# Splitting the gate and up signals of a fused attention and FFN kernel, with satisfied waits on two engines

## The chip, the cores and the metric

The kernel runs on one core of one Trainium2 chip. The metric is device time in microseconds of one execution; the *span* is the part from the first to the last instruction that the profile covers. I call reported time minus span the *surplus*. Spans are listed to 0.1 us for every run, so a surplus read from them is good to about 0.05 us.

## The reference, cut to what matters

```python
x = A_x                                              # [1, 2048, 640] bf16
g = sigmoid((x * gate_w).sum(-1, keepdims=True))
a = linear_attention(x, wqkv, w_phi, wo)             # 32 heads of 20, softmax features
b = (silu(x @ w_gate) * (x @ w_up)) @ w_down         # FFN width 1728
return g * a + (1 - g) * b
```

## The kernel before

The kernel is written by hand for five engines. A small tracker gives each engine one semaphore, lets every recorded operation raise it by one, and puts the waits that the data need ahead of an operation. A group of matmuls signals once, at its last one. A list of short codes fixes the order of all work.

The part that the change touches is one FFN item: the gate half and the up half of a 128-column block, each five matmuls of 512 columns into its own PSUM bank of a pair (PSUM: the `ps` tiles of the profile, into which the matmuls write). ScalarE takes the Tanh of the gate bank and copies the up bank, VectorE forms (tanh + 1) * gate, and POOL multiplies that with the copy.

```python
def fitem(bt, k):
    pr = next_pair()
    ...
    if k < 13:
        g, up = bank(2 * pr, 0, 512), bank(2 * pr + 1, 0, 512)
        mm(group(g, [(wg[:, c, P * k:P * k + P], xr[c]) for c in range(5)])
           + group(up, [(wu[:, c, P * k:P * k + P], xr[c]) for c in range(5)]))
        h = hT[:, buf, k, :]
    ...
    actop(h, g, ACTF.Tanh, 0.5)
    actop(u, up, ACTF.Copy)
    stt(h, h, 1.0, g, ALU.add, ALU.mult)
    tt("pool", h, h, u, ALU.mult)
```

`H` in the order is a pair of warm-up matmuls, `U` a part of a value tile, `M` premultiplies a block of the key weights (`wT`), `K` is a key projection, `N` ends the accumulation of keys times values, `Z` follows it.

The softmax here doesn't subtract the row's maximum and nothing guards it: scores larger than these inputs give would overflow.

## Time and profile before

| | before |
|---|---|
| time, median of 3 runs (range) | 289.55 us (289.07 to 290.51) |
| span of the profiled run | 288.40 us |
| TensorE busy | 285.0 us, 99% |
| last matmul starts | 286.30 us |
| first key projection to last matmul | 266.96 us |
| instructions of PE, of ScalarE | 4042, 300 |

The instruction counts take a matmul as two, weight load and multiply (1975 of each on the page). The stretch from the first key projection to the last matmul is the difference of two start times in the trace (19.34 and 286.30). The *tail* is the stretch from the start of the last matmul to the end of the span. The prediction shows the lines of this profile and how they are read.

### The profile page before, as it was taken

How to read it: one execution, taken by the hardware profiler on the slowest of the kernel's cores; microseconds unless marked ns; L12 is line 12 of the kernel's file. 1: busy time of each engine (PE TensorE's matmuls, PEld its weight loads, DVE VectorE, ACT ScalarE, POOL GpSimd, SP SyncE). 2: the span in 40 equal slices, each digit the busy share in tenths (PEclk: the TensorE clock that was granted, in tenths of full speed). 3: DMA queues.
4: the chain of work that ended last, by engine and by line, in shares of the span. 5: the costliest groups of instructions: out<-in, count | busy, mean ns of one | idle time of the engine just before them, and what ended most of it. 6: DMA issues, size and time to landing. Idle time of an engine off the chain costs nothing.

```text
span 288.4 us, 4897 instructions
## 1 busy us (share of the span) xinstructions
PE 285.0 (99%) x1975; PEld 174.6 (61%) x1975; DVE 162.6 (56%) x243; ACT 148.2 (51%) x252; POOL 160.4 (56%) x125
## 2 busy tenths in 40 slices
PE   8999999999999999999999999999999999999997
PEld 6667777575644445556775556675554446656776
DVE  2146748486468987669992385980317799200000
ACT  1468768676674556673355663225675452234112
POOL 8286899889545799835743348350653649601000
DMA  7975779000010497302383002061020004410101
GB/s 212 178 115 120 111 197 375 26 1 2 0 50 0 84 323 135 78 5 44 56 140 91 15 1 50 2 142 49 2 50 0 2 1 84 91 45 0 49 23 48
DMA packets 48943, 21.62 MB, mean 75 GB/s; under 512 B 39384, under 2 KB 48792, under 8 KB 48920
## 3 DMA queue, kind: packets, MB, share of 16 engines
q1 hardware_dynamic: 48190, 20.62, 31.4%
q10 hardware_dynamic: 730, 0.68, 0.7%
q8 instruction: 16, 0.26, 0.4%
q14 instruction: 7, 0.06, 0.1%
HBM read 9.29 MB, written 2.62 MB: 41 GB/s over the span
## 4 chain that ended last, share of the span: by engine, by line
PE 93%; SPq 4%; DMA 2%; issue 0%; DVE 0%
PE ps L294 93%; SPq L347 3%; DMA wT<-in_A_wqkv_dram 2%; SPq L348 1%; DVE osb L724 0%; PE ps L306 0%
## 5 line engine op out<-in xcount | busy, mean ns | idle before, releaser
L322 POOL TENSOR_TENSOR hT<-hT,us 128x512 bf16<-128x512 bf16 (+1 forms) x56 | 65.6, 1180 | 66.3 <-DVE hT L326 66.1
L326 DVE SCALAR_TENSOR_TENSOR hT<-hT,ps 128x512 bf16<-128x512 bf16 (+1 forms) x56 | 37.5, 683 | 73.0 <-ACT hT L312 60.7
L294 PE MATMUL ps<-xT,wg 128*128 128x512 bf16 x260 | 64.6, 379 | 0.0
L294 PE MATMUL ps<-xT,wu 128*128 128x512 bf16 x260 | 64.6, 379 | 0.0
L294 PE MATMUL ps<-wd,hT 128*128 128x320 bf16 (+2 forms) x462 | 63.9, 295 | 0.0
L312 ACT ACTIVATE hT<-ps 128x512 bf16<-128x512 f32 (+2 forms) x60 | 35.8, 596 | 46.6 <-PE ps L294 46.4
L322 POOL TENSOR_TENSOR ph<-eq,qc 128x1320 bf16<-128x1320 bf16 x16 | 42.3, 2646 | 26.1 <-DVE qc L632 24.0
L294 PEld LDWEIGHTS ps<-wd,hT 128*128 128x128 bf16 x462 | 44.5, 98 | 17.5 <-issue 0.2
L294 PE MATMUL ps<-wqk,xT 128*128 128x320 bf16 x320 | 47.7, 299 | 0.1
L294 PEld LDWEIGHTS ps<-xT,wu 128*128 128x128 bf16 x260 | 25.5, 98 | 30.7
L294 PEld LDWEIGHTS ps<-xT,wg 128*128 128x128 bf16 x260 | 25.1, 98 | 27.8 <-ACT oT L312 0.8
L312 ACT ACTIVATE osb<-ps,omg 128x640 bf16<-128x640 f32 (+2 forms) x17 | 12.9, 757 | 53.7 <-PE ps L294 53.7
L322 POOL TENSOR_TENSOR ekr<-ekr,krec 128x1280 bf16<-128x1280 bf16 x16 | 37.4, 2357 | 5.2 <-DVE krec L336 5.2
L294 PEld LDWEIGHTS ps<-wqk,xT 128*128 128x128 bf16 x320 | 30.6, 98 | 13.2 <-ACT us L312 0.5
L312 ACT ACTIVATE us<-ps 128x512 bf16<-128x512 f32 (+1 forms) x56 | 33.2, 594 | 0.3 <-POOL hT L322 0.2
L312 ACT ACTIVATE eq<-ps 128x640 bf16<-128x640 f32 x32 | 22.3, 703 | 17.3 <-POOL ph L322 10.4
L333 DVE TENSOR_REDUCE ksum<-ekr 128x64 f32<-128x1280 bf16 x16 | 23.5, 1470 | 11.2 <-ACT ekr L312 11.2
L312 ACT ACTIVATE ekr<-ps 128x640 bf16<-128x640 f32 x32 | 22.3, 703 | 8.2 <-PE ps L294 7.7
L333 DVE TENSOR_REDUCE qz<-eq 128x64 f32<-128x1280 bf16 x16 | 23.7, 1478 | 2.2 <-ACT eq L312 2.2
L294 PE MATMUL ps<-wvg,xT 128*128 128x320 bf16 (+1 forms) x160 | 24.4, 301 | 0.3 <-DVE xT L318 0.2
L294 PE MATMUL ps<-wog,oT 128*128 128x320 bf16 (+2 forms) x165 | 24.7, 295 | 0.0
L333 DVE TENSOR_REDUCE qw<-ez 128x64 f32<-128x1280 bf16 x16 | 23.6, 1476 | 0.0
(73 smaller groups left out, 188.4 us busy)
## 6 DMA issues: line engine op xcount, KB each, us to landing
out_dram<-osb SPq DMA_DIRECT2D x15, 160.0 KB, 1.9
wd<-in_B_w_down_dram SPq DMA_DIRECT2D x1, 2080.0 KB, 10.7
wg<-in_B_w_gate_dram SPq DMA_DIRECT2D x1, 1040.0 KB, 11.3
wu<-in_B_w_up_dram SPq DMA_DIRECT2D x1, 1040.0 KB, 11.5
wg<-in_B_w_gate_dram SPq DMA_DIRECT2D x1, 800.0 KB, 7.4
wu<-in_B_w_up_dram SPq DMA_DIRECT2D x1, 800.0 KB, 9.0
wog<-in_A_wo_dram SPq DMA_DIRECT2D x2, 375.0 KB, 7.3
wvg<-in_A_wqkv_dram SPq DMA_DIRECT2D x4, 160.0 KB, 4.1
```

What stands on the lines that cost most here:

```text
L294: last = pe.matmul(o, lhsT=l, rhs=r, start=st, stop=sp_, skip_group_check=sk)
L312: return run("act", lambda: act.activation(o, i, func, scale=scale), rd, [o])
L322: return run(e, lambda: eo.tensor_tensor(o, a, b, op), [a, b], [o])
L326: return run("dve", lambda: dve.scalar_tensor_tensor(out=o, in0=a, scalar=s, in1=b, op0=op0, op1=op1), rd, [o])
L333: return run("dve", lambda: dve.tensor_reduce(o, i, AX.X, ALU.add), [i], [o])
L347: return eo.dma_start_transpose(dst, src)
L348: return eo.dma_start(dst, src)
```

## The change

It does two things. The gate half of an FFN item now signals by itself, so that the Tanh need not wait for the up half. And waits that are already satisfied are put into the programs of ScalarE (88, code `a`) and PE (24, in `N`). They make the programs longer (on net, PE's from 4042 to 4046 instructions and ScalarE's from 300 to 360) and so shift the program fetches: the last packet of queue 8, which I take for PE's, began at 285.44 us before.

```diff
+NWAIT = 88
+NPEW = 24
-H0 H1 H2 H3 H4 H5 H6 H7 H8 H12 G ...
+H0 H1 a H2 H3 H4 H5 H6 H7 H8 H12 G ...
+    def act_waits():
+        for _ in range(NWAIT):
+            act.wait_ge(tr.sem["pe"], 1)
...
-            mm(group(g, [(wg[:, c, P * k:P * k + P], xr[c]) for c in range(5)])
-               + group(up, [(wu[:, c, P * k:P * k + P], xr[c]) for c in range(5)]))
             h = hT[:, buf, k, :]
+            mm(group(g, [(wg[:, c, P * k:P * k + P], xr[c]) for c in range(5)]))
+            mm(group(up, [(wu[:, c, P * k:P * k + P], xr[c]) for c in range(5)]))
...
     def kv_end():
+        for _ in range(NPEW):
+            pe.wait_ge(tr.sem["pe"], 1)
         kv_finish()
```

More of the change, by code (lines that the diff above doesn't have):

```diff
@@ L36 @@
 ORDER = """
-H0 H1 H2 H3 H4 H5 H6 H7 H8 H12 G X0 H9 H10 U0.0 X1 H11 U1.0 U0.1 U1.1 X2 U2.0 U0.2 U1.2 U2.1
+H0 H1 a H2 H3 H4 H5 H6 H7 H8 H12 G X0 H9 H10 U0.0 X1 H11 U1.0 U0.1 U1.1 X2 U2.0 U0.2 U1.2 U2.1
 X3 U2.2 U0.3 U1.3 U2.3 U0.4 U1.4 U2.4 V3 Y F0.1 M1 i3 M0 F0.0 M2 V4 M3 M4 K0 K1 I S0 V6 V5 S1 P0
@@ L744, in _build @@
         "f": lambda i: load_ffn(FCUT[i], FCUT[i + 1]), "L": load_late_weights, "T": tail_weights, "J": gates,
-        "Y": w_blocks, "I": kv_begin, "N": kv_end, "Z": z_row,
+        "Y": w_blocks, "a": lambda: act_waits(), "I": kv_begin, "N": kv_end, "Z": z_row,
         "Q": qtile, "A": qsum, "B": qden, "C": qscale, "c": qmul,
```

## The prediction

One paragraph is cut from the text where marked: statements about the hardware that go beyond what this case's runs show. The trace of before: 91 wait instructions on PE and 41 on ScalarE; sixteen packets of 16384 bytes on queue 8, which begin when 229 to 4005 of PE's instructions have started, 252 apart on average; packets of 8192 bytes on queue 14. The pace from which the text counts its 13 late steps, N/2.4 + 2.5 ns for N columns, is here a line through this trace's median steps: it is within 1 ns of them at 80, 96, 140, 224, 320 and 512 columns (35, 42.5, 61, 96, 136 and 216 ns) and 3 ns below them at 63 and 321. Of the three stretched issues named under (b), the one of 2.58 us is a plain load of gate weights and no transpose.

> **What bounds the kernel now.** I read the page from the top: busy shares, the slices, the queues, the chain that ended last.
>
> ```profile
> PE 285.0 (99%) x1975; PEld 174.6 (61%) x1975; DVE 162.6 (56%) x243; ACT 148.2 (51%) x252; POOL 160.4 (56%) x125
> ...
> PE   8999999999999999999999999999999999999997
> ...
> q8 instruction: 16, 0.26, 0.4%
> q14 instruction: 7, 0.06, 0.1%
> ...
> PE 93%; SPq 4%; DMA 2%; issue 0%; DVE 0%
> ```
>
> TensorE is busy 99% of the span, and no slice but the first and the last is below 9. The other engines are little more than half busy. The two instruction lines are the program fetches that the change wants to place. Busy TensorE can still be padded, so I cut the span at the two places where the chain changes hands and asked for busy time in each stretch:
>
> ```profile
> 0.00:19.00 19.00, 17.58 (x141) 12.05 (x141) 5.83 (x14) 8.00 (x17) 10.98 (x28) 1.00 0.82 175
> 19.00:286.50 267.50, 267.40 (x1834) 162.57 (x1834) 156.41 (x229) 140.17 (x237) 149.42 (x98) 1.00 0.29 68
> 286.50:288.40 1.90, 0.01 (x1) 0.00 (x0) 0.32 (x1) 0.00 (x0) 0.00 (x0) 1.00 0.19 45
> ```
>
> First number: length; second: TensorE busy. The middle 267.5 us are full. From the trace's start times, the median step from a 512-column matmul to the next is 216 ns and from a 320-column one 136 ns, and between 19 and 286.5 us only 13 steps are more than 15 ns over N/2.4 + 2.5 ns; their excess is 1.06 us in all. So this stretch has about 1 us to give. The chain in order of time shows what sets its two ends:
>
> ```profile
> 14.36 4.61 DMA wT<-in_A_wqkv_dram
> 18.97 0.05 issue
> 19.02 59.32 PE ps L294 x562
> ...
> 128.49 158.03 PE ps L294 x1020
> 286.52 0.02 issue
> 286.54 0.32 DVE osb L724
> ```
>
> The start is SyncE's row of transposing loads, whose last weight block lands at 18.97. The end is the eviction of the last 96 columns and their store: issued by ScalarE at 286.89, its semaphore complete at 288.35. The reported time is 289.64 for the profiled run against a span of 288.40; I carry that 1.24 us over unchanged.
>
> [...] the last fetch ran from 285.44 to 286.42, and of the store then under way (128x320) fifteen arrivals came by 286.11 and the sixteenth at 287.49.
>
> **The change part by part.**
>
> *Split signal.* No matmul is removed, added or moved; the order of matmuls, activations and vector operations is the same. The last gate matmul now signals too, so the Tanh of a gate bank may start 5 x 216 ns = 1.08 us earlier, while the up half runs. The first consumer of a pair frees its banks sooner. What is that worth? Only where TensorE waits for such a bank. Of the 13 steps, ten surround the attention output groups (about 95 ns before and after each, tied to waits for transposed phi and to switches of operand). One is 78 ns at 131.07, after a wait for oT. The largest, 239 ns, is an FFN bank:
>
> ```profile
> 127.03 0.60 ACT L312 ACTIVATE hT<-ps 128x512 bf16<-128x512 f32 x1 [0.72 <-PE ps L294]
> 127.52 0.59 ACT L312 ACTIVATE us<-ps 128x512 bf16<-128x512 f32 x1
> 127.66 0.69 DVE L326 SCALAR_TENSOR_TENSOR hT<-hT,ps 128x512 bf16<-128x512 bf16 x1 [0.70 <-ACT hT L312]
> ...
> 128.46 2.57 PEld L294 LDWEIGHTS ps<-wqk,xT 128*128 128x128 bf16 x20 [0.53 <-ACT us L312]
> ```
>
> The next projection wants the pair; VectorE's product with the gate bank ends at 127.66 + 0.69 = 128.35, and the weight load starts 0.11 us later. With the split, this Tanh starts after the two activations that end near 126.3, not at 127.03; the product is then done by about 127.6 and the 0.24 us go. TensorE has no slack behind it, so they reach the end: **-0.24 us**. The new waits are cheap: the us copies get their own wait for PE, 16 of them as extra instructions on ScalarE, executed while its Tanh of 596 ns runs: 0.
>
> *88 waits on ScalarE.* In the built program two waits share one instruction, so they are 44. The trace has one pair of such instructions in a row on ScalarE, 87 ns apart: 44 x 87 ns = 3.83 us. They stand after its five loads (last one issued 2.74 to 3.19) and before the table load:
>
> ```profile
> 5.01 1.28 ACT L312 ACT_TABLE_LOAD   x1 [5.01 <-POOL v1r L340]
> ...
> 9.82 0.71 ACT L312 ACTIVATE v1r<-ps 128x640 bf16<-128x640 f32 x1 [3.53 <-PE ps L294]
> ```
>
> 3.19 + 3.83 = 7.02; plus 1.28 and a little is 8.3, and the first activation is wanted at 9.82. Slack 1.5 us, cost 0. Even at 110 ns each they end in time.
>
> *24 waits on PE.* They become 12 instructions at the end of the K/V stage (about 78 us). Consecutive ones on PE start 110 ns apart: 12 x 0.11 = 1.32 us of sequencer time. The sequencer runs ahead: the two nearest event instructions ran at 75.23 and 78.49, and the matmuls behind them started at 76.81 and 80.39, 1.6 and 1.9 us later. So 1.32 us fit, narrowly: 0, at worst +0.3 us. On net the PE program grows by 4 instructions, since the split turns eight other event instructions into waits carried by a matmul and adds one early.
>
> *Fetches.* Everything behind the 12 waits moves by 4 places, so the last PE fetch comes about 4 instructions, some 0.1 us, earlier. Today it delays one sixteenth of a store to 287.49, but the last store lands at 288.35 without a straggler: 0.86 us slack, gain about 0. ScalarE's first fetch moves by 44 instructions, to somewhere in the loading stage, and one of its later fetches into the quiet middle. An 8192-byte fetch takes 0.31 us on one DMA engine. At worst it delays the last weight block by that much: 0 to +0.3 us. At the start the first PE fetch (14.45 to 15.41) meets the last weight transpose: SyncE's issue of it took 2.11 us where its neighbours took 1.28. TensorE then lost 0.22 + 0.52 us waiting for wT. The change shifts the PE program there by one instruction only, so I keep this loss.
>
> Sum: 289.55 - 0.24 + (0 to 0.3 PE waits) + (0 to 0.3 start) - (0 to 0.2 tail) is 289.1 to 289.9; I take **289.3 us**, because the costs are the less likely terms.
>
> **The rivals.** (a) *The waits become the bound.* If the twelve PE waits are not hidden, TensorE idles up to 1.3 us near 78 us, or a late table load shifts the start. For it: only 1.6 us of lead. Against: 91 event instructions today leave almost no gap. Time: 290 to 290.8. (b) *Fetch placement is worth more than I think.* If the loss at the start goes (0.74 us) and the tail gains some tenths besides, the time is 288.3 to 288.7. For it: stretched transposes wherever a fetch falls (issues of 2.11, 2.30 and 2.58 us beside fetches at 14.45, 28.26 and 39.80). Against: early PE fetches hardly move, and the last store has no straggler. (c) *The split frees TensorE broadly.* ScalarE is idle 46 us before Tanh, POOL 66 us before the h product. But all of that idles beside a full TensorE; the ceiling is the 1.06 us of gaps: 288.5. (d) *Earlier release collides:* an earlier Tanh and product move VectorE and POOL work onto other buffers, and a new small wait appears; then 289.6.
>
> **Range and chances.** All terms together can hardly move the time by 1.5 us; 2% is 5.8 us. The three runs before spread from 289.07 to 290.51, so a median of a few runs carries some 0.4 us of its own. Range 288.6 to 290.0. Faster by over 2%: 0.01; within 2%: 0.985; slower: 0.005.
>
> **What would show it.** Right: TensorE still 99%, the stretch from about 19 us to the last matmul 267.2 to 267.5 us long; the step near 128 us back to 216 ns; ScalarE's table load ending near 8.3 us and its first activation still near 9.8; no gap near 78 us; the Tanh group's idle before it smaller without effect on TensorE; the last PE fetch near 285.3. Wrong if: the last weight block lands clearly before or after 18.97, a gap of over 0.3 us opens behind the PE waits, or the stretch from the last matmul to the end changes from 1.9 us by more than 0.3.

## The result, and the profile after

The changed kernel takes 289.94 us (median of 6 runs, 289.45 to 290.48) against 289.59 us for before (6 runs, 289.07 to 290.51). The ratio is 1.0008, with a 95% interval of 0.9988 to 1.0029: the same. A ratio here is the mean time of one kernel's fast runs over that of the other's of the same rounds, so it isn't quite the ratio of the medians.

First the page after: busy shares, the two instruction queues, and the chain that ended last.

```profile
PE 284.9 (99%) x1975; PEld 174.8 (61%) x1975; DVE 163.5 (57%) x243; ACT 151.6 (53%) x252; POOL 159.8 (55%) x125
...
q8 instruction: 16, 0.26, 0.4%
q14 instruction: 8, 0.07, 0.1%
...
PE 98%; ACT 1%; DVE 0%; issue 0%; ACTq 0%
```

I take queue 8 for PE's program: it had 16 packets in the span with 4042 and 4046 PE instructions, and 15 with 4034 (split_only) and 4030 (before_short). Queue 14 I take for ScalarE's, among others. It has one packet more: at 228.35 us, when 318 of ScalarE's instructions have started, where before had only 300. And SyncE and its loads have left the chain; ScalarE has entered it. The chain in order of time (start, length, what) says where:

```profile
8.40 1.39 PE ps L296 x10
...
9.95 1.28 ACT L314
11.24 0.01 issue
11.25 0.71 ACT v1r L314
11.95 0.07 ACT svec L314
12.02 0.07 issue
12.10 66.26 PE ps L296 x616
```

An unnamed ScalarE instruction of 1.28 us stands in the path of a TensorE that was thought never to wait for ScalarE. The timeline of that window (start, length, engine, line, operation; in brackets the idle time before it and what ended it) names it:

```profile
9.95 1.28 ACT L314 ACT_TABLE_LOAD   x1 [9.95 <-PE ps L296]
...
11.25 0.71 ACT L314 ACTIVATE v1r<-ps 128x640 bf16<-128x640 f32 x1
...
12.10 1.24 PE L296 MATMUL ps<-xT,wg 128*128 128x512 bf16 x5 [0.40 <-ACT svec L314]
```

The table load waited for TensorE, and moved from 5.01 to 9.95 us. The first activation moved from 9.82 to 11.25, and TensorE had to wait for the PSUM bank that it frees: from the matmul at 11.40 to the next is 0.56 us more than that matmul takes. On the other side, the split does what it is for. The same FFN item near 127 us, after:

```profile
126.23 0.59 ACT L314 ACTIVATE hT<-ps 128x512 bf16<-128x512 f32 x1
126.85 0.69 DVE L328 SCALAR_TENSOR_TENSOR hT<-hT,ps 128x512 bf16<-128x512 bf16 x1 [0.70 <-ACT hT L314]
...
128.36 2.56 PEld L296 LDWEIGHTS ps<-wqk,xT 128*128 128x128 bf16 x20 [0.41 <-issue]
```

The Tanh starts while the up half still runs, the product ends at 127.54 instead of 128.35, and the projection no longer waits for it. The excess of a step is what it takes beyond the usual pace of these traces, the line N/2.4 + 2.5 ns for N columns (medians 216 ns at 512 and 136 ns at 320, in both). From start times, the excess of the step at 128 us fell from 239 to 94 ns and the 78 ns one at 131 us is gone. From the first key projection to the last matmul it is now 266.75 us: **0.21 us less**. The groups of instructions show what became of ScalarE's waiting, before Tanh and before the copy of the up bank (`us`). Before, then after (count, busy us, mean ns, idle before):

```profile
L312 ACT ACTIVATE hT<-ps 128x512 bf16<-128x512 f32 (+2 forms) x60 | 35.8, 596 | 46.6 <-PE ps L294 46.4
...
L312 ACT ACTIVATE us<-ps 128x512 bf16<-128x512 f32 (+1 forms) x56 | 33.2, 594 | 0.3 <-POOL hT L322 0.2
```

```profile
L314 ACT ACTIVATE hT<-ps 128x512 bf16<-128x512 f32 (+2 forms) x60 | 35.8, 597 | 16.0 <-PE ps L296 15.8
...
L314 ACT ACTIVATE us<-ps 128x512 bf16<-128x512 f32 (+1 forms) x56 | 33.5, 598 | 19.2 <-PE ps L296 18.2
```

Of the thirty microseconds that ScalarE no longer waits before Tanh, nineteen came back before the copies, which now wait for the up half by themselves. The idle time of ScalarE has moved more than shrunk (138 us before, 134 after, summed over its groups), and 0.21 us of time came of it.

### The profile page after: what moved, and what is told of

Same layout as the page of the kernel before. It is cut to its first block, busy times and chain, and to the rows that moved or that the text cites. A ratio compares the mean times of both kernels' runs of the same rounds, so it can differ in the third digit from the quotient of the medians.

```text
span 288.2 us, 4961 instructions
## 1 busy us (share of the span) xinstructions
PE 284.9 (99%) x1975; PEld 174.8 (61%) x1975; DVE 163.5 (57%) x243; ACT 151.6 (53%) x252; POOL 159.8 (55%) x125
## 4 chain that ended last, share of the span: by engine, by line
PE 98%; ACT 1%; DVE 0%; issue 0%; ACTq 0%
PE ps L296 97%; PE ps L478 1%; PE ps L308 1%; ACT L314 0%; ACT v1r L314 0%; DVE xT L320 0%; DVE osb L730 0%; ACTq L139 0%; ACT svec L314 0%
```

## The experiments

My theory after the result: the split is worth 0.21 us; the ScalarE waits lose up to 0.56 us at the start through the table load; the PE waits are hidden. The rival is the change's own idea, that the place of the last fetches matters. The table has what is read from each run. "PE" and "ACT" count instructions of the two programs. Surpluses are means with their ranges; the surplus of the kernel before was 1.19 to 1.28 us in all of its 44 runs beside these.

| run | PE / ACT | median us, before beside it | ratio (95%) | median span | surplus |
|---|---|---|---|---|---|
| after_again | 4046 / 360 | 290.08, 289.57 | 1.0010 (0.9977 to 1.0043) | 288.85 | 1.24 (1.21 to 1.28) |
| split_only | 4034 / 316 | 289.76, 289.57 | 1.0001 (0.9965 to 1.0036) | 287.85 | 1.64 (1.28 to 2.12) |
| waits_only | 4054 / 344 | 290.52, 289.57 | 1.0031 (0.9996 to 1.0066) | 289.25 | 1.25 (1.24 to 1.28) |
| table_first | 4046 / 361 | 289.53, 289.57 | 0.9999 (0.9965 to 1.0033) | 288.3 | 1.24 (1.21 to 1.28) |
| split_pe_waits | 4046 / 316 | 289.92, 289.45 | 1.0014 (0.9997 to 1.0031) | 288.5 | 1.36 (1.20 to 1.43) |
| split_act_waits | 4034 / 361 | 289.88, 289.45 | 1.0016 (1.0001 to 1.0032) | 288.35 | 1.74 (1.40 to 2.15) |
| pe_dose | 4082 / 316 | 294.30, 289.45 | 1.0166 (1.0145 to 1.0187) | 292.9 | 1.36 and 1.43 |
| two_act_waits | 4034 / 317 | 290.53, 289.45 | 1.0036 (1.0014 to 1.0058) | 289.05 | 1.56 and 1.41 |
| table_first_2 | 4046 / 361 | 289.56, 289.41 | 1.0002 (0.9981 to 1.0023) | 288.35 | 1.23 (1.20 to 1.27) |
| before_short | 4030 / 300 | 289.86, 289.41 | 1.0021 (0.9996 to 1.0046) | 288.6 | 1.24 (1.20 to 1.29) |
| few_act_waits | 4046 / 327 | 290.03, 289.41 | 1.0022 (1.0001 to 1.0042) | 288.8 | 1.23 (1.21 to 1.25) |
| before_window | 4035 / 300 | 290.28, 289.70 | 1.0034 (1.0011 to 1.0056) | 288.95 | 1.38 (1.22 to 1.59) |

All gave correct results. Each had 6 timed runs, pe_dose and two_act_waits 2; before had 11 beside each group.

### The halves of the change

**split_only**: no added wait.

```diff
-NWAIT = 88
-NPEW = 24
+NWAIT = 0
+NPEW = 0
```

> The split signal alone, without any added wait. My theory: only the middle stretch gains. The step near 128 us falls from 239 ns over its share to about 94 ns and the 78 ns one near 131 us vanishes, so matmuls between 20 us and the end have 0.83 us of excess instead of 1.06. ScalarE's table load is back at about 5 us and its first activation at 9.8, so TensorE stops at 18.5 us only for the weight block, not at 11.4 for ScalarE. Time 0.2 us under before, ratio 0.9993, not to be told from 1 by timing alone. The last PE fetch, eight places later, starts near 285.4 to 285.7. Rival (the fetches are what mattered): without the waits the tail from the last matmul to the end grows by 0.2 us or more over the 2.06 us of the changed kernel.

The stretch is 266.75 us, the table load is at 5.01 us, and nothing stops TensorE near 11.4 us. That part holds. But the expected place of the last PE fetch was wrong:

```profile
q8 instruction: 15, 0.25, 0.3%
q14 instruction: 7, 0.06, 0.1%
```

The sixteenth PE packet is not late; it has left the span. Its straggling store has gone too (the 128x320 store has all its arrivals by 285.48, no lone one 1.4 us later), yet the stretch from the last matmul to the end is 2.09 us where it was 2.10 before. So the straggler never set the end. What did grow is the surplus: 1.28 to 2.12 us against 1.19 to 1.28. The kernel's span has the lowest median of the table and its time is no better than before's.

**waits_only**: the joined signal put back, both sets of waits kept.

```diff
+            mm(group(g, ...) + group(up, ...))
             h = hT[:, buf, k, :]
-            mm(group(g, ...))
-            mm(group(up, ...))
```

> Both sets of waits, without the split. My theory: no gain anywhere. The gaps of 239 and 78 ns near 128 and 131 us stay; the table load sits behind the matmuls of the first value tile, at about 9.9 us; TensorE stops about 0.5 us near 11.4 us; no gap near 76 us. Time equal to before within 0.3 us, or 0.1 to 0.5 us above it, depending on when the last weight block lands. Rival (placed fetches pay): 0.3 us or more under before.

The trace is as expected: the stretch is 266.96 us, the gaps near 128 and 131 us are back (243 and 75 ns), the table load is at 10.27 us, and TensorE stops for 0.62 us at 11.71. The time is not: the median is 0.95 us above before, where at most 0.5 was expected, though the interval of the ratio still holds 1. The waits alone are a loss, if anything.

**after_again**: the changed kernel, unaltered.

> The changed kernel again on the chip of the other three. Both theories: table load near 9.95 us, stop of TensorE near 11.4 us of about 0.5 us, last PE fetch near 285.2 us, tail 2.06 us; time 289.5 to 290.3 and within 0.3% of before. What tells: where its start (first projection of keys) lies against that of split_only and table_first on the same chip. My theory has it 0 to 0.5 us later than theirs.

Table load at 10.51 us, stop of 0.56 us at 11.95. The last weight block landed at 17.97 us, the earliest of all fourteen traces, and TensorE did not wait for it: here nothing hid the stop. Its first key projection is at 19.92 us, against 18.92 in split_only and 19.34 in table_first.

### Why the table load is late

**two_act_waits**: two satisfied waits on ScalarE instead of 88, none on PE.

```diff
-NWAIT = 88
-NPEW = 24
+NWAIT = 2
+NPEW = 0
```

> Split signal with only two satisfied waits on ScalarE (one more instruction than the split alone) and none on PE. My theory: what costs at the start is not the 44 instructions (they are over by 6.5 us) but the order they give to the conditions: the wait for the first value tile's matmuls goes ahead of the table load. So the table load is at about 10 us here too, the first activation at 11.3 to 11.8, and TensorE stops for about 0.56 us near 11.4 to 12. Rival (the number of waits delays the load): table load near 5 us, no stop.

The ScalarE timeline of this run:

```profile
10.52 1.28 ACT L314 ACT_TABLE_LOAD   x1 [10.52 <-PE ps L296]
11.81 0.71 ACT L314 ACTIVATE v1r<-ps 128x640 bf16<-128x640 f32 x1
```

One more instruction does the same as 44 (load at 10.52 us, 9.95 in the changed kernel), so their number is not the cause. The built programs show the cause, and the traces agree. The first activation collects conditions: its own (PE at 34, POOL at 15) and the added ones (PE at 1). In these builds only one stays on the activation; the others are in wait instructions ahead of it; and the table load is between those and the activation. Before, POOL's condition went ahead (wait at 4.96 us, load at 5.01) and "PE at 34" stayed (the activation waits for PE until 9.82). With added waits a "PE at 1" stays, and "PE at 34", the end of the first value tile's matmuls, goes ahead of the table load too (in the changed kernel the last two waits are at 9.81 and 9.89 us, the load at 9.95).

**table_first**: one tiny activation ahead of the waits, so that the table is loaded before them.

```diff
     def act_waits():
+        c0 = nc.const_aps.tensor(1.0, [P, 1], F32)
+        run("act", lambda: act.activation(omg[:, 0:1], c0, ACTF.Exp), [], [omg[:, 0:1]])
         for _ in range(NWAIT):
```

> The changed kernel with one tiny Exp activation put ahead of ScalarE's waits, so that the table is loaded before them. My theory: table load at about 3.3 us, waits until about 8 us, first value activation at 9.8 us, no stop of TensorE at 11.4 us; it again waits for the weight blocks near 16.3 and 18.5 us. So the start is set by the weight transposes alone and the time is 0 to 0.5 us under the changed kernel. Rival (the late table load is wholly hidden): same stretch from the first projection of keys to the end and the same start, no difference at all.

```profile
3.23 1.28 ACT L428 ACT_TABLE_LOAD   x1 [3.23 <-issue]
```

The load is early and the stop at 11.4 us is gone. On the same chip the median span is 288.3 us against 288.85 for after_again, and the median time 289.53 against 290.08: 0.55 us, the size of the stop. The intervals of the ratios overlap, so the timing alone would not carry this; the stop in four traces (after, after_again, waits_only, two_act_waits) and its absence here do. In the first profile of the changed kernel nearly all of the loss was hidden (first key projection at 19.36 us, before at 19.34): there the last weight block came at 18.49 us, and TensorE, already late, no longer had to wait for it as it did before (0.50 us).

### Are the PE waits free?

**pe_dose**: split, 96 PE waits, none on ScalarE.

```diff
-NWAIT = 88
-NPEW = 24
+NWAIT = 0
+NPEW = 96
```

> Split signal with four times the PE waits (48 instructions) and none on ScalarE. My theory: 48 x 0.11 = 5.2 us of the sequencer against a lead of about 1.6 us before Z, plus what it has queued: TensorE now stops near 78 us for 2 to 4 us, and the time rises by as much, to 291.5 to 293.5. The 12 instructions of the change were thus hidden, not free. Rival (waits run beside the queue whatever their number): no stop, time as split with PE's waits. The last PE fetch moves about 36 places earlier, to about 284 us.

TensorE's timeline:

```profile
75.22 2.88 PE L296 MATMUL ps<-wqk,xT 128*128 128x320 bf16 x20
80.82 0.21 PE L308 MATMUL ps<-ident,zh 120*128 120x120 bf16 x1 [2.71 <-DVE svec L332]
80.87 1.95 PE L296 MATMUL ps<-xT,wg 128*128 128x512 bf16 x5
82.61 2.27 PE L296 MATMUL ps<-xT,wu 128*128 128x512 bf16 x5
84.71 1.46 PE L296 MATMUL ps<-xT,wt 128*128 128x512 bf16 x6
```

The row names a VectorE instruction as releaser, but the wait instructions run almost without a break from 75.52 to 80.71 us, about 0.106 us apart, and the matmul starts when they are over: it is the sequencer. The stretch grew from 266.75 to 271.31 us. Of these 4.56 us, 2.88 are the stop; the rest are the matmuls after it, which for 3.4 us start 427 ns apart instead of 216; the trace's record of the granted clock reads 0.5 from 81.26 to 84.68 us. That was not foreseen, and with it the time, 294.30 us, passed the 291.5 to 293.5 expected. With 12 instructions (75.77 to 77.09 us in the changed kernel, with Z's transpose at 78.19 and no gap) nothing is lost. They are hidden, not free.

### Where a fetch costs

**split_pe_waits**: split and PE's waits.

```diff
-NWAIT = 88
+NWAIT = 0
```

> Split signal with PE's waits alone; ScalarE as in the split alone, with its late fetch still after the span. The split alone reported times 1.28 to 2.12 us above its spans where every other kernel had 1.19 to 1.29. Theory P (PE's sixteenth fetch, pushed past the end by eight missing instructions, costs that): the sixteenth packet is back at about 285.2 us and the reported time is 1.2 to 1.3 us above the span in all six runs. Theory A (ScalarE's fetch at 289.25 costs it): the surplus stays at 1.3 to 2.1 us. Both: table load at 5 us, no stop of TensorE at 11.4 us, no gap near 76 us, 266.75 us from the first key projection to the last matmul; span 287.5 to 288.3 in the median. Under P this is the best kernel so far, 0.3 us or so under before.

**split_act_waits**: table_first without PE's waits.

```diff
-NPEW = 24
+NPEW = 0
```

> Split signal with ScalarE's waits behind an early table load, without PE's waits. ScalarE's third fetch lies near 228 us inside the span; PE's sixteenth is past the end and missing from the records of the span. Theory P: the reported time is 1.3 to 2.1 us above the span, varying from run to run. Theory A: 1.2 to 1.3 us in all six runs. Both: table load near 3.2 us, 266.75 us from first key projection to last matmul, tail of the span without the store's straggler (all of the 128x320 store's arrivals within 0.2 us).

Neither theory P nor theory A holds alone. With PE's fetch back in the span (285.72 us), the surplus is 1.36 us, above 1.28 in four of six runs, with one 8192-byte packet at 290.06 us, 1.22 us after the span. With ScalarE's fetch back in the span (228.08 us) it is 1.74 us, and now the missing PE packet shows: 16384 bytes at 289.31 us, 1.34 us after the span's end. By these two runs both engines' fetches are paid when they fall behind the span, PE's by about 0.5 us and ScalarE's by about 0.12 (means, less 1.24). The packet records agree with this in the one profiled run of each kernel: the late packet ends 1.79, 1.54, 1.72 and 2.31 us after the span in split_only, split_pe_waits, pe_dose and split_act_waits, and the surpluses of those runs are 1.45, 1.28, 1.43 and 1.97, always some 0.3 us less. In two_act_waits this fails (packet end 0.55, surplus 1.56); there the PE packet is not in the records, so the last fetch isn't seen. (It is in no record of split_only either.) The median spans here are above before's, 288.2 us on this chip, and the expected lead over before did not come.

**before_short**: the kernel before, three warm-up pairs fewer.

```diff
-H0 H1 H2 H3 H4 H5 H6 H7 H8 H12 G ...
+H0 H1 H2 H3 H4 H5 H12 G ...
```

> The kernel before with three of its 13 warm-up pairs of matmuls left out, so that its PE program is 12 instructions shorter (4030 against 4042) and nothing else changes. My theory: as in the split alone, the sixteenth PE fetch leaves the span, and the reported time is 1.4 to 2.1 us above the span instead of 1.24, though no signal was split and ScalarE's program is untouched. Gaps of 239 and 78 ns near 128 and 131 us stay. Rival (the surplus comes from the split's signals or from ScalarE's longer program): surplus 1.2 to 1.3 us. The span itself may lose a little at the start from fewer warm-up matmuls.

A miss. PE's fetch left the span (15 packets), and yet the surplus is 1.24 us. "Outside the span" is thus not what is paid for.

**before_window**: two warm-up pairs fewer.

```diff
-H0 H1 H2 H3 H4 H5 H6 H7 H8 H12 G ...
+H0 H1 H2 H3 H4 H5 H6 H12 G ...
```

> The kernel before with two warm-up pairs left out: 4035 PE instructions, between the 4034 at which the surplus appeared and the 4042 of before. With three pairs out (4030) the sixteenth fetch left the span and yet nothing was paid, so my theory as it stood has fallen. [...] Then at 4035 the surplus of time over span is 1.4 to 2.1 us in most runs though only one warm-up pair is added to the kernel that paid nothing, and a sixteenth PE packet may show after the span's end. Rival (the surplus belongs to the split or to ScalarE's 316 instructions): 1.2 to 1.3 us, as at 4030 and 4042. The stretch from first key projection to last matmul stays at 266.96 us.

What is cut there was the author's guess at the reason, which no trace shows; the expected surplus of 1.4 to 2.1 us at 4035 instructions rested on that guess. With five instructions more than before_short the surplus is 1.38 us: 1.59, 1.51 and 1.41 in three runs, 1.29, 1.28 and 1.22 in the others. No run of the kernel before had over 1.28. So it appears without any split and with ScalarE's program untouched, and only in a narrow range of lengths: not at 4030 and not at 4042, but at 4034 and 4035. It is smaller here than I expected and not in most runs. The sixteenth packet is in no record of this run. The surplus is also the smaller part of its loss: of the 0.58 us by which the median time lies above before's, 0.45 are in the span.

**few_act_waits**: table_first with 20 waits on ScalarE.

```diff
-NWAIT = 88
+NWAIT = 20
```

> The early-table version with 20 waits (10 instructions) on ScalarE instead of 88. ScalarE's program then has 327 instructions; its third fetch, which came after about 318, falls inside the span but near its end, between 281 and 287 us, while the last stores run. My theory: the surplus over the span is 1.24 us as with 88 waits, since only a fetch after the end is paid; the early place near 228 us brings nothing more. Rival (a fetch beside the last stores delays them): the tail from the last matmul to the end grows from 2.1 by 0.3 us or more, or the surplus stays at 1.36.

The surplus is 1.21 to 1.25 us in the six runs with 327 ScalarE instructions, where 316 gave 1.36. The tail is 2.09 us. The place was a miss: no packet of queue 14 starts after 267.18 us, so the fetch is some 20 us before the end and not beside the last stores. For the surplus, the 88 waits of the change do no more than 20 would. The time is no gain all the same: the median is 0.62 us above before's, with an interval just clear of 1, and the median span is 288.8 us against 288.2. The one profile is of its fastest run and does not show why.

**table_first_2**: table_first again, on another chip.

> The changed kernel with the early table load, a second time, as the version that should keep the gain of the split and pay neither for the late table load nor for late fetches. My theory: 266.75 us from first key projection to last matmul (0.21 under before), surplus of the time over the span 1.24 us as before, no stop at 11.4 us; median time 0 to 0.4 us under before. Rival (the split's 0.21 us is eaten at the start by the weight blocks, which land when they land): time equal to before within 0.1 us.

289.56 against 289.41 us: the same. The stretch is 266.75 us and the surplus 1.23, so the 0.21 us are there, and by this profile the start takes them back: it has its first key projection at 19.58 us, with a wait of 0.18 us for the last weight block.

## Why the prediction was right or wrong

The time (289.3 predicted, 289.94 measured) lies in the range and the class was right, for the reason given first: TensorE is full from 19 us on, so ScalarE and POOL had nothing to win. That it lies inside the upper end, 290.0, by 0.06 us is luck: the next six runs of the same kernel (after_again) gave 290.08. Point by point:

- **Split signal, -0.24 us**: right in mechanism. Measured 266.96 to 266.75 us, -0.21; that this is so near in size is partly luck. The step at 128 us keeps 94 ns of excess, like other steps beside the attention output groups, so it gave 0.145 us and not 0.24; the 78 ns step at 131 us, which I had not counted, went as well. The steps around those groups were also misread: they are eleven and not ten, and four of them are of some 20 ns.
- **ScalarE's waits, cost 0**: this step failed. "Plus 1.28 and a little is 8.3" took for granted that the table load follows the waits at once. The wait instructions, of two waits each, took 77 ns and all but the last two were done by 6.5 us, better than I assumed; but the order of conditions tied the table load to TensorE, 9.95 us, and stopped TensorE for 0.56 us. This could have been read from the built program, which shows the table load behind waits for PE and POOL, and before only behind POOL. I had allowed 0 to 0.3 us at the start, for another reason, ScalarE's first fetch among the loads. Of that nothing is seen: with this fetch at 11.0 to 12.6 us (six traces) the last weight block landed at 17.97 to 19.20 us, in the eight other traces at 18.00 to 20.23.
- **PE's waits, 0, at worst +0.3**: right; no gap near 76 us, and pe_dose shows that the margin is real but finite.
- **Fetches, gain about 0**: right for the pair of kernels compared, for an incomplete reason. The straggling store doesn't matter, as said; the last PE fetch came at 285.16 (predicted 285.3). But I asked only what moving today's fetch by 0.1 us gives, and not what the split alone would do to it. It takes eight instructions off PE's program and adds 16 to ScalarE's, and so, as far as the packets show it, moves both engines' last fetch behind the span, at 0.4 us in the mean (1.64 less 1.24). The waits take that back. "I carry that 1.24 us over unchanged" came true only because of them.
- **Rival (a)**, in its second form "a late table load shifts the start", is what happened; its 290 to 290.8 us just misses the first median and just holds that of after_again. **Rival (b)** was half right: fetch placement is worth something, but against the split alone and not against before. Its other half, the first PE fetch that meets the last weight transposes, was not tried. The kept traces bear on it: in all fourteen, the one transposing issue of SyncE beside that fetch took 1.85 to 2.68 us, where most take 1.28. In twelve it was a load of weights; in after_again and waits_only, where the fetch began at 14.74 and 15.25 us, it was the load behind them. And the loss to win was 0.50 us and not 0.74: at 16.5 us TensorE lost nothing, the step there being 220 ns where 216 is full pace.

The balance against before: -0.21 from the split, 0 from the PE waits, 0 in the surplus, and 0 to +0.56 at the start, according to how late the last weight block is. The measured difference of 0.35 us in the medians is at the upper end of that, and the 0.51 of after_again beyond it; neither is clear of noise.

What stays open: why the first key projection varies between 18.79 and 20.60 us over the traces, which is more than any effect of the change; whether table_first beats before by its 0.21 us, which runs of this spread can't tell; why few_act_waits, which has neither the stop nor the surplus, is 0.62 us above before; and why the surplus of a late fetch varies from run to run (1.40 to 2.15 us in split_act_waits).

## What to carry to other kernels

On a kernel whose bound engine is full, look for the few steps where that engine waits and value a change by those alone: here 30 us less waiting before Tanh, most of which came back before the copies, were worth 0.21 us. A change of a few instructions had effects outside its arithmetic: on which condition stays with an instruction (table load from 5.01 to 9.95 us) and, it seems, through the length of PE's program (mean surplus 1.24 us at 4030 instructions, 1.38 at 4035, at most 1.28 at 4042). So compare the built programs, the span, and the reported time less the span. An inserted "free" wait was only as free as the lead of the sequencer (12 wait instructions on PE left no gap, 48 stopped TensorE for 2.88 us), and on ScalarE it moved the table load behind it.

## What these traces measured of fetches, waits and the clock

- The packets of queue 8 are 16384 bytes; those of queue 14 are 8192, and in the changed kernel the three that I take for ScalarE's come when 54, 190 and 318 of its instructions have started, 136 and 128 apart. A fetch just behind the span seems not to be hidden: surplus up to 2.15 us (split_act_waits) against 1.24, though before_short had none.
- One wait instruction held two conditions in these builds (88 waits were 44 instructions on ScalarE, 24 were 12 on PE, 96 were 48), and the table load came behind the one that waits for the first value tile: at 9.95 us, where it was at 5.01 before.
- An instruction of two satisfied waits took 77 ns on ScalarE and 105 to 111 ns on PE, from start to start, back to back; one on PE took 135.
- In pe_dose a stop that adds 2.88 us was followed by steps of 427 ns at 512 columns, for 3.4 us, with a granted clock of 0.5.
